# One transfer for the first load, and the last values ahead of the fold, in an adaLN decode block with cached attention

## The chip, the cores and the metric

The kernel runs on one core of a Trainium2 chip. The metric is the device time of one execution in microseconds (us), the median of several runs.

## The reference

Two decode tokens (B = 2, one position each) of width 512 go through an adaLN block: attention over a cache of 4096 keys with 32 heads of 128, then a dense layer with Mish, both behind a layer norm that is scaled and shifted by a condition `c`. Cut to what matters:

```python
mod = (silu(c) @ w_mod).reshape(2, 6, 1, 512)          # w_mod: 512 x 3072
sa, ca, ga, sb, cb, gb = (mod[:, i] for i in range(6))
h = layernorm(x) * (1 + ca) + sa
q = (h @ wq)                                            # wq: 512 x 4096, 32 heads of 128
scores = einsum("bhqd,bhkd->bhqk", q, k_cache) * 128 ** -0.5
o = einsum("bhqk,bhkd->bhqd", softmax(scores), v_cache) # caches: 2 x 32 x 4096 x 128
x = x + ga * (o @ wo)                                   # wo: 4096 x 512
h = layernorm(x) * (1 + cb) + sb
x = x + gb * (mish(h @ w1 + b1) @ w2)                   # w1: 512 x 1376, w2: 1376 x 512
```

Everything is float32. The caches alone are 268 MB; all that is read once is 297 MB.

## The kernel before

**The loads.** Nearly all input comes in 36 loads, which `stream` lays out ahead of time: each is one or more transfers into a "room", a tile of 128 partitions x 16384 floats (8 MB, 64 KB a partition). There are three rooms (`bufs=3`), so load n + 3 has to wait until a room has been read. Loads 1 to 31 are one transfer each, with rows of 64 KB: the keys of a head and, in what room is left, values and projection weights. Load 0 holds the weights of modulations 0 and 1, the first two query projections and the keys of head 0; it is two transfers with rows of 32 KB, weights first. Load 32 has values of head 28, the last `wo` pieces and modulation 2's weights; load 33 the values of heads 29 and 30; load 34 modulation 4's weights and the values of head 31 in three transfers; load 35 the weights of modulations 3 and 5, `w1` and `w2` in six transfers, cut so that the last `w2` chunks come in small pieces. All loads go through SyncE's queue (SP), in this order, issued by `load` (L140); `used` calls it when everything in an older room has been used.

**Three small transfers** go through ScalarE's queue at the start: `cq` (the condition, L162), `xq` (x, L162; eight rows of 512 B each) and `bias` (b1 in columns, L164; 128 rows of 48 B).

**The start.** On TensorE (PE), in program order: `cps` (c turned into columns, L237), the two sums of the first layer norm (L210, L218), `fps` (L269: the bias b1 put into PSUM, where the hidden layer is added at the very end), modulations 0 and 1 (L247), `hps` (L237), and the first two query projections (L294). The engine works strictly in that order.

**The middle.** For each of 32 heads VectorE (DVE) multiplies the keys by the query in place (`products`, L321) and sums over 128 (`sums`, L324), 64 keys a partition; PE and ScalarE (ACT) make the soft-max and PE multiplies by the values (`weighted_v`, L362), with four groups of 32 rows side by side. After four heads `value_sums`, `head_values` and `project_o` bring the result through `wo` into `att`.

**The tail.** Behind the last head: the values of heads 29 and 30, then `project_o` for all but head 31, a copy of `att` to SBUF (`att_sb`, L470), the first half of head 31's values, the fold (L474: four 32-row groups brought together into `xps`), modulation 4, kept by ACT through `keep`, the second half of the values, their way through `value_sums`, `head_values` and `head_out_q` (L401), which adds head 31 into `xps`. Then x is updated (L490, L493), the second layer norm follows (`centred`, `rstd`), modulation 3, `w1` (L514), Mish, modulation 5 and `w2` (`yps`, L554). `busy(n)` (L301) is n idle matmuls of 128 columns, which only keep PE going.

The order on each engine is the order of the program: there is no planner.

Of the kernel before, what the change touches and what calls it, by code (L numbers as in the profile page):

```python
# [9 lines left out]
AF = mybir.ActivationFunctionType  # L10
ALU = mybir.AluOpType
# [7 lines left out]
BIG = 8192  # L19
W = 2048  # L20
# [6 lines left out]
ROW = 2 * BIG  # L27


def stream():  # L30


    order, n_v = [], 0
    for h in range(1, HEADS):
        order.append(("k", h))
        if h % HC == HC - 1 and HC < h < HEADS - 1:
            c = (h + 1) // HC
            order.append([("wq", c), ("wo", c - 2)])
        if h not in AHEAD:
            order += [("v", n_v, 0), ("v", n_v, 1)]  # L40
            n_v += 1
    order = [x if isinstance(x, list) else [x] for x in order]

    def size(x):
        return sum(SIZES[key[0]] for key in x)

    loads = [[([("m01", 0), ("wq", 0), ("wq", 1)], (4 * W,)), ([("k", 0)], (BIG,))]]
    for _ in range(1, HEADS):
        row = []
        while size(row) < ROW:  # L50
            room = ROW - size(row)
            row += order.pop(next(i for i, x in enumerate(order) if size(x) <= room))
        loads.append([(row, (ROW,))])
    last = [("v", h, i) for h in range(HEADS - 4, HEADS) for i in range(2)]
    assert order == [[key] for key in last[:2]], order
    loads += [
        [(last[:2] + [("wo", 6), ("wo", 7), ("m2", 0)], (BIG + 3 * W,))],
        [(last[2:4], (BIG,)), (last[4:6], (BIG,))],
        [([("m4", 0)] + last[6:], (W + HALF, W, W))],
        [  # L60
            ([("m3", 0), ("w1", 0)], (W + 2 * sum(WIDTHS), 2 * sum(WIDTHS))),
            ([("m5", 0), ("w2", 0)], (W + 5 * 512, 4 * 512, 512, 512)),
        ],
    ]
    return loads
# [3 lines left out]
def kernel(  # L69
# [15 lines left out]
    nc = tc.nc  # L85
# [7 lines left out]
    H = HEADS  # L93
# [12 lines left out]
    def small_ps(name):  # L106
        return psum.tile([P, 512], F32, tag="sm", name=name, bufs=2)

    def wide_ps(name):
        return psum.tile([P, 512], F32, tag="mm", name=name, bufs=2)  # L110
# [19 lines left out]
    w_t = {}  # L130
# [14 lines left out]
    def used(*keys):  # L145

        nonlocal loaded
        done.update(keys)
        while loaded < len(loads) and (
            loaded < 3 or all(key in done for keys, _ in loads[loaded - 3] for key in keys)  # L150
        ):
            load(loaded)
            loaded += 1
# [6 lines left out]
    for t, src in ((cq, head[0]), (xq, head[1])):  # L160
        nc.gpsimd.memset(t, 0.0)
        nc.scalar.dma_start(out=t[::TB, :], in_=src)  # L162
    bias = const.tile([P, NCH + 1], F32, name="bias")
# [7 lines left out]
        out=fold, in_=ident.rearrange("p (g r) -> p r g", g=G), axis=AX.X, op=ALU.add  # L171
# [3 lines left out]
        out=mean_w, in0=fold[:, None, :].to_broadcast([P, G, R]), scalar1=1.0 / D, scalar2=None, op0=ALU.mult  # L175
# [4 lines left out]
        out=half, in_=ident.rearrange("p (b r) -> p r b", b=B), axis=AX.X, op=ALU.add  # L180
# [19 lines left out]
    def centred(src, name, first_sum=None, between=None):  # L200

        rs = const.tile([P, 8], F32, name=f"rs_{name}")
        xc = work.tile([P, P], F32, tag="xc", name=f"xc_{name}", bufs=1)
        sq = work.tile([P, P], F32, tag="sq", name=f"sq_{name}", bufs=1)
        if first_sum is None:
            nc.vector.tensor_reduce(out=rs[:, 0:1], in_=src, axis=AX.X, op=ALU.add)
        else:
            first_sum(rs[:, 0:1])
        mps = small_ps(f"mean_{name}")
        nc.tensor.matmul(mps[:, 0:1], lhsT=mean_w, rhs=rs[:, 0:1], start=True, stop=True)  # L210
        nc.vector.tensor_scalar(out=xc, in0=src, scalar1=mps[:, 0:1], scalar2=None, op0=ALU.subtract)
        nc.vector.scalar_tensor_tensor(
            sq, xc, 1.0, xc, op0=ALU.mult, op1=ALU.mult, accum_out=rs[:, 1:2]
        )
        if between is not None:
            between()
        vps = small_ps(f"var_{name}")
        nc.tensor.matmul(vps[:, 0:1], lhsT=mean_w, rhs=rs[:, 1:2], start=True, stop=True)  # L218
        return xc, vps[:, 0:1], rs
# [20 lines left out]
    def modulation(name, n, t, ps=None, ks=range(G)):  # L240


        if ps is None:
            ps = wide_ps(f"modps{name}")[:, : n * P].rearrange("p (m n) -> p m n", m=n)
        for k in ks:
            for g in range(G):
                nc.tensor.matmul(  # L247
                    ps[R * g : R * (g + 1)],
                    lhsT=ct[:, k, :],
                    rhs=t[:, k, :].rearrange("p (m n) -> p m n", m=n)[:, :, P * g : P * (g + 1)],  # L250
                    start=(k == 0),
                    stop=(k == G - 1),
                )
        return ps
# [9 lines left out]
    xc, var, rs = centred(xq, "a")  # L264
# [10 lines left out]
    mod = {}  # L275

    def keep(m, ps):
        mod[m] = const.tile([P, P], F32, name=f"mod{m}")
        nc.scalar.copy(mod[m], ps)
# [17 lines left out]
    def busy(n):  # L297

        for lo in range(0, n, 2):
            cols = P * min(2, n - lo)  # L300
            nc.tensor.matmul(ov[1][:, :cols], lhsT=ident, rhs=e_t[0].rearrange("p c m -> p (c m)")[:, :cols], start=True, stop=True)  # L301
# [56 lines left out]
    def weighted_v(h, part, bank, first=True, last=True):  # L358

        for c in range(NB // 2):  # L360
            g = c % G
            nc.tensor.matmul(  # L362
                ov[bank][R * g : R * (g + 1), :],
                lhsT=e_t[h % HC][:, NB // 2 * part + c, :],
                rhs=v_t[h, part][:, c, :],
                start=(first and part == 0 and c < G),
                stop=(last and part == 1 and c >= NB // 2 - G),
            )
        used(("v", h, part))

    def value_sums(bank, copies):

        o_t.clear()
        n = 4 // len(copies)
        for i, copy in enumerate(copies):
            o = work.tile([P, 4, DH], F32, tag="o", name=f"o{bank}")[:, :n]
            copy(o.rearrange("p m d -> p (m d)"), ov[bank][:, n * DH * i : n * DH * (i + 1)])  # L377
            for m in range(n):
                o_t[n * i + m] = o[:, m, :]

    def head_values(n, i0=0, i1=HC):
        x = slice(B * i0, B * i1)
        tps = small_ps(f"otp{n}_{i0}")
        for m in range(4):
            nc.tensor.matmul(  # L385
                tps[:, x], lhsT=o_t[m], rhs=pick_t[n][:, m, x], start=(m == 0), stop=(m == 3),
            )
        nc.scalar.copy(ot_t[n % 2][:, i0:i1, ::TB], tps[:, x].rearrange("p (i b) -> p i b", b=B))
# [9 lines left out]
    def head_out_q(h):  # L398

        for g in range(G):  # L400
            nc.tensor.matmul(  # L401
                xps[R * g : R * (g + 1), :P],
                lhsT=ot_t[h // HC % 2][:, h % HC, :],
                rhs=wo_t[h // HC][:, h % HC, P * g : P * (g + 1)],
                start=False, stop=(h == H - 1), skip_group_check=True,
            )
# [51 lines left out]
    N = H // HC - 1  # L458
# [10 lines left out]
    att_sb = work.tile([P, 512], F32, tag="o", name="att_sb")  # L469
    nc.scalar.copy(att_sb, att)  # L470
    xps = psum.tile([P, 512], F32, tag="att", name="xps", bufs=1)
    weighted_v(H - 1, 0, 1 - N % 2)
    for g in range(G):
        nc.tensor.matmul(  # L474
            xps[R * g : R * (g + 1), :P], lhsT=fold, rhs=att_sb[:, P * g : P * (g + 1)],
            start=True, stop=False, skip_group_check=True,
        )
    keep(4, modulation("4", 1, w_t["m4"])[:, 0, :])
    weighted_v(H - 1, 1, 1 - N % 2)
    value_sums(1 - N % 2, (nc.scalar.copy, nc.vector.tensor_copy))  # L480
    busy(2)
    head_values(N, HC - 1, HC)
    busy(1)
    head_out_q(H - 1)
    wm3, wm5 = w_t["m3"], w_t["m5"]
    w1_t, w2_t = w_t["w1"], w_t["w2"]

    xg = work.tile([P, P], F32, tag="sq", name="xg", bufs=1)
    x2 = const.tile([P, P], F32, name="x2")
# [3 lines left out]
        nc.vector.scalar_tensor_tensor(x2, xg, 1.0, xq, op0=ALU.mult, op1=ALU.add, accum_out=total)  # L493

    m4 = work.tile([P, P], F32, tag="xn", name="m4", bufs=1)
    busy(2)
    xc, var, rs = centred(x2, "b", add_x, lambda: busy(4))
    mps3 = modulation("3", 1, wm3)
    busy(1)
    nc.vector.scalar_tensor_tensor(m4, mod[4], 1.0, xc, op0=ALU.add, op1=ALU.mult)  # L500
    y0, y1 = rstd(var, rs)
    nc.scalar.activation(xc, m4, AF.Copy, scale=y0)
    nc.vector.scalar_tensor_tensor(hq, xc, y1, mps3[:, 0, :], op0=ALU.mult, op1=ALU.add)
# [63 lines left out]
def _lay_out(np, a):  # L567
# [39 lines left out]
    for n, parts in enumerate(stream()):  # L607
        for i, (keys, widths) in enumerate(parts):
            row = np.concatenate([piece(*key) for key in keys], axis=1)
            cuts = np.split(row, np.cumsum(widths)[:-1], axis=1)  # L610
            for j, t in enumerate(cuts):
                arrays[f"load{n}_{i}_{j}"] = np.ascontiguousarray(t)
# [25 lines left out]
```

## Time and profile before

| what | value |
|---|---|
| time, median of 3 runs | 698.67 us (698.63 to 698.77) |
| the profiled execution's own time | 698.77 us |
| its span | 696.9 us |
| busy: PE / DVE / ACT / POOL | 41% / 84% / 6% / 1% |
| DMA | 297.48 MB in 6690 packets, mean 427 GB/s |
| mean granted clock of PE | 0.677 |

The profile is of one execution; its span runs from the first instruction to the last, and the execution's own time is 1.9 us longer. Times in the lines are microseconds from the span's start, unless marked as nanoseconds. In a timeline a line has the start, the duration, the engine, the line of the kernel, the operation, the tile written and the tiles read, the count, and in brackets the idle time before it with what ended it; PEld is the weight load of PE, and SPq and ACTq are the queues of DMA issues. "DMA to landing" is the time from a transfer's issue to its last completion. In a line of a window (`A:B`) stand its length, the busy time of PE, PEld, DVE, ACT and POOL with counts, then the granted clock of PE, the DMA share and GB/s.

### The profile page before, as it was taken

To read this page: it belongs to the slowest core of one execution; us is meant where nothing else is said; L and a number is where in the kernel's file an instruction comes from. 1 tells how busy PE (TensorE), PEld (TensorE's weight loads), DVE (VectorE), ACT (ScalarE), POOL (GpSimd) and SP (SyncE) were. 2 spreads that over 40 slices of the span, in tenths; PEclk is the share of its full clock that TensorE was granted. 3 is DMA by queue.
4 is the path that set the end of the run, shared out by engine and by line. 5 is a ranking of instruction groups with operands and counts; after the bars stand their busy time and mean duration, and the time that the engine had idled before them with its cause. 6 is when DMAs were issued, how large, how long until landed. Compare 5 with 4: busy or idle time off the path is not lost.

```text
span 696.9 us, 3922 instructions
## 1 busy us (share of the span) xinstructions
PE 284.6 (41%) x1640; PEld 103.9 (15%) x1640; DVE 587.1 (84%) x219; ACT 44.3 (6%) x169; POOL 4.2 (1%) x20
## 2 busy tenths in 40 slices
PE   0603334335145615234342806234333425224697
PEld 0200011001011201101110301011101111001245
DVE  3399999999999999999999999999999999899002
ACT  1000000000000000000000000000000000000011
POOL 2000000000000000000000000000000000000000
PEclk9966656768565567656575656656575658556889
DMA  9999999999999999999999999999999999999996
GB/s 388 455 421 421 425 467 429 418 430 425 463 422 421 437 421 456 429 421 441 421 451 429 418 444 425 448 426 421 441 429 445 429 421 441 429 434 422 425 419 266
DMA packets 6690, 297.48 MB, mean 427 GB/s; under 512 B 888, under 2 KB 912, under 8 KB 1168
## 3 DMA queue, kind: packets, MB, share of 16 engines
q1 hardware_dynamic: 6496, 297.21, 98.9%
q8 instruction: 13, 0.21, 0.1%
q10 hardware_dynamic: 176, 0.01, 0.0%
q14 instruction: 5, 0.04, 0.0%
HBM read 297.22 MB, written 0.00 MB: 426 GB/s over the span
## 4 chain that ended last, share of the span: by engine, by line
DMA 63%; DVE 33%; PE 2%; issue 0%; SPq 0%; POOL 0%; ACT 0%; ACTq 0%; DVEq 0%; POOLq 0%
DMA room<-in_load 61%; DVE room L321 16%; DVE s L324 16%; DMA bias<-in_b1c 3%; PE ov L362 1%; PE qps L294 1%; PE modps L247 1%; PE yps L554 0%; SPq L140 0%; DVE m L337 0%; DVE hcw L283 0%; DVE m L329 0%; PE fps L269 0%; ACT q L295 0%; ACTq L162 0%
## 5 line engine op out<-in xcount | busy, mean ns | idle before, releaser
L321 DVE TENSOR_TENSOR room<-room,q 128x8192 f32<-128x8192 f32 x32 | 278.1, 8691 | 40.0 <-DMA room<-in_load 35.5
L324 DVE TENSOR_REDUCE s<-room 128x64 f32<-128x8192 f32 x32 | 277.9, 8683 | 0.0
L362 PE MATMUL ov<-room,e 128*32 128x512 f32 x1024 | 177.0, 841 | 73.5 <-ACT e L340 31.2
L333 PE MATMUL mt<-d,same 128*128 128x64 f32 x64 | 18.7, 388 | 194.0 <-DVE d L331 194.0
L362 PEld LDWEIGHTS ov<-room,e 128*32 128x32 f32 x1024 | 39.8, 146 | 180.8 <-issue 128.3
L340 ACT ACTIVATE e<-s,m 64x64 f32<-64x64 f32 x64 | 22.1, 345 | 547.9 <-DVE m L337 547.1
L333 PEld LDWEIGHTS mt<-d,same 128*128 128x128 f32 x64 | 13.5, 263 | 224.6 <-DVE d L331 177.6
L294 PE MATMUL qps<-room,hcw 128*128 128x512 f32 x64 | 40.7, 797 | 4.6 <-DMA room<-in_load 3.8
L348 PE MATMUL l<-l,ones 128*128 128x8 f32 x16 | 4.6, 359 | 73.7 <-ACT e L340 73.7
L385 PE MATMUL otp<-pick,o 128*128 128x8 f32 (+2 forms) x72 | 14.4, 328 | 37.3 <-ACT o L377 35.4
L377 DVE COPY o<-ov 128x256 f32<-128x256 f32 x1 | 0.4, 423 | 25.1 <-ACT o L377 25.1
L385 PEld LDWEIGHTS otp<-pick,o 128*128 128x128 f32 x72 | 13.6, 282 | 46.6 <-ACT o L377 43.7
L294 PEld LDWEIGHTS qps<-room,hcw 128*128 128x128 f32 x64 | 15.9, 261 | 24.4 <-issue 18.6
L348 PEld LDWEIGHTS l<-l,ones 128*128 128x128 f32 x16 | 3.8, 296 | 75.1 <-ACT e L340 75.1
L393 PE MATMUL att<-room,ot 128*32 128x512 f32 x62 | 10.9, 756 | 5.2 <-DMA room<-in_load 4.7
L337 DVE TENSOR_REDUCE m<-mt 128x1 f32<-128x64 f32 x32 | 6.9, 217 | 6.3 <-PE mt L333 6.3
L340 ACT ACTIVATION_READ_ACCUMULATOR e<-s,m 64x1 f32 x64 | 11.8, 185 | 0.0
L331 DVE TENSOR_SCALAR d<-half,m 128x64 f32<-128x64 f32 x32 | 8.1, 254 | 1.1
L273 DVE SCALAR_TENSOR_TENSOR hq<-modps,xn 128x128 f32<-128x128 f32 x1 | 0.3, 291 | 10.4 <-PE modps L247 10.4
L247 PE MATMUL modps<-room,ct 128*32 128x128 f32 (+1 forms) x160 | 8.1, 346 | 0.0
L329 DVE TENSOR_REDUCE m<-s 128x1 f32<-128x64 f32 x32 | 6.9, 217 | 0.9
L377 ACT COPY o<-ov 128x512 f32<-128x512 f32 (+1 forms) x9 | 5.1, 562 | 24.2 <-PE ov L362 24.1
(100 smaller groups left out, 68.5 us busy)
## 6 DMA issues: line engine op xcount, KB each, us to landing
room<-in_load SPq DMA_DIRECT2D x4, 4096.0 KB, 28.5
room<-in_load SPq DMA_DIRECT2D x1, 7168.0 KB, 39.1
room<-in_load SPq DMA_DIRECT2D x1, 3072.0 KB, 26.1
room<-in_load SPq DMA_DIRECT2D x3, 1024.0 KB, 22.3
room<-in_load SPq DMA_DIRECT2D x1, 2400.0 KB
room<-in_load SPq DMA_DIRECT2D x1, 2304.0 KB, 20.3
room<-in_load SPq DMA_DIRECT2D x1, 1376.0 KB, 15.2
room<-in_load SPq DMA_DIRECT2D x2, 256.0 KB, 22.6
```

The costliest lines, as they stand in the source:

```text
L247: nc.tensor.matmul(ps[R * g : R * (g + 1)], lhsT=ct[:, k, :], rhs=t[:, k, :].rearrange("p (m n) -> p m n", m=n)[:, :, P * g : P * (g + 1)] ...
L294: nc.tensor.matmul(ps, lhsT=hcw[:, k, :], rhs=wq_t[ch][:, k, :], start=(k == 0), stop=(k == G - 1))
L321: nc.vector.tensor_tensor(out=k_t[h], in0=k_t[h], in1=qv, op=ALU.mult)
L324: nc.vector.tensor_reduce(out=s_t[h], in_=k_t[h], axis=AX.X, op=ALU.add)
L329: nc.vector.tensor_reduce(out=m_t[h][:, 0:1], in_=s_t[h], axis=AX.X, op=ALU.max)
L331: nc.vector.tensor_scalar(out=d, in0=half, scalar1=m_t[h][:, 0:1], scalar2=None, op0=ALU.mult)
L333: nc.tensor.matmul(mps[h], lhsT=same, rhs=d, start=True, stop=True)
L340: nc.scalar.activation(e_t[i][own_b, :, M * i + 4 * b : M * i + 4 * b + 4], s_t[h][own_b].rearrange("p (c m) -> p c m", m=4), AF.Exp, bias ...
L348: nc.tensor.matmul(lps[n], lhsT=ones, rhs=sum_t[n % 2], start=True, stop=True)
L362: nc.tensor.matmul(ov[bank][R * g : R * (g + 1), :], lhsT=e_t[h % HC][:, NB // 2 * part + c, :], rhs=v_t[h, part][:, c, :], start=(first a ...
L385: nc.tensor.matmul(tps[:, x], lhsT=o_t[m], rhs=pick_t[n][:, m, x], start=(m == 0), stop=(m == 3),)
L393: nc.tensor.matmul(att[R * i : R * (i + 1), :], lhsT=ot_t[n % 2][:, i, :], rhs=wo_t[n][:, i, :], start=(n == 0), stop=(n == H // HC - (2 i ...
```

## The change

Two things are changed. Load 0 becomes a single transfer with rows of 64 KB, in the same order of content. In the tail both halves of head 31's values are multiplied one after the other, and `value_sums` follows at once; the fold comes behind them. Modulation 4 moves behind that and is cut in two: k = 0 and 1 ahead of `head_out_q`, k = 2 and 3 behind it, where idle matmuls stood. It is no longer kept in SBUF as such: ACT writes 1 + modulation straight into `m4`, and DVE multiplies that by the centred x. Of the idle matmuls of 128 columns in the part shown here, 5 remain (1 + 3 + 1) of 10 (2 + 1 + 2 + 4 + 1).

```diff
-    loads = [[([("m01", 0), ("wq", 0), ("wq", 1)], (4 * W,)), ([("k", 0)], (BIG,))]]
+    loads = [[([("m01", 0), ("wq", 0), ("wq", 1), ("k", 0)], (ROW,))]]
...
-    weighted_v(H - 1, 0, 1 - N % 2)
+    for part in range(2):
+        weighted_v(H - 1, part, 1 - N % 2)
+    value_sums(1 - N % 2, (nc.scalar.copy, nc.vector.tensor_copy))
     for g in range(G):
         nc.tensor.matmul(
             xps[R * g : R * (g + 1), :P], lhsT=fold, rhs=att_sb[:, P * g : P * (g + 1)],
             start=True, stop=False, skip_group_check=True,
         )
-    keep(4, modulation("4", 1, w_t["m4"])[:, 0, :])
-    weighted_v(H - 1, 1, 1 - N % 2)
-    value_sums(1 - N % 2, (nc.scalar.copy, nc.vector.tensor_copy))
-    busy(2)
+    busy(1)
     head_values(N, HC - 1, HC)
-    busy(1)
+    mps4 = modulation("4", 1, w_t["m4"], ks=(0, 1))
     head_out_q(H - 1)
+    modulation("4", 1, w_t["m4"], mps4, (2, 3))
...
     m4 = work.tile([P, P], F32, tag="xn", name="m4", bufs=1)
-    busy(2)
-    xc, var, rs = centred(x2, "b", add_x, lambda: busy(4))
+    nc.scalar.activation(m4, mps4[:, 0, :], AF.Copy, bias=1.0)
+    xc, var, rs = centred(x2, "b", add_x, lambda: busy(3))
     mps3 = modulation("3", 1, wm3)
     busy(1)
-    nc.vector.scalar_tensor_tensor(m4, mod[4], 1.0, xc, op0=ALU.add, op1=ALU.mult)
+    nc.vector.tensor_tensor(out=m4, in0=xc, in1=m4, op=ALU.mult)
     y0, y1 = rstd(var, rs)
```

## The prediction

> **What bounds the kernel now.** I read the page first, for the engines and the DMA by slices, then the chain that ended last, then the timeline of the first 50 us and of the last 35.
>
> ```profile
> DMA  9999999999999999999999999999999999999996
> GB/s 388 455 421 421 425 467 429 418 430 425 463 422 421 437 421 456 429 421 441 421 451 429 418 444 425 448 426 421 441 429 445 429 421 441 429 434 422 425 419 266
> q1 hardware_dynamic: 6496, 297.21, 98.9%
> DMA 63%; DVE 33%; PE 2%; issue 0%; SPq 0%; POOL 0%; ACT 0%; ACTq 0%; DVEq 0%; POOLq 0%
> ```
>
> The DMA engines are busy in every slice but the last, all 297 MB on SP's queue. The 33% of DVE in the chain misleads; a stretch of the chain in order of time (start, duration, what) shows why:
>
> ```profile
> 102.08 38.23 DMA room<-in_load
> 140.34 8.69 DVE room L321
> 149.13 8.70 DVE s L324
> 157.83 0.02 SPq L140
> 157.89 40.51 DMA room<-in_load
> 198.42 8.69 DVE room L321
> ```
>
> A load of 8 MB is issued when DVE has read a room (157.83) and lands two load times later (198.40), because another load is still ahead of it. Three loads land between 140.31 and 198.40, one every 19.36 us, while DVE needs 17.4 us and a little for a head. So the stream of loads is the bound, and a load's issue matters only if the queue ahead of it has run dry. That leaves two places to look at: whether the queue can run dry, and what follows the last landing.
>
> **Part 1, the first load as one transfer of 64 KB rows.** Its own bytes are the same. These rows show the start: SP's loads, the queues in the first 25 us, two windows (the last number is GB/s), and the timeline up to the first pass of DVE.
>
> ```profile
> L140 SPq DMA_DIRECT2D room<-in_load x4: 392/422/495, 0.7 to 2.1; - x4
> DMA to landing us min/median/max: 21.6/40.5/59.4
> ```
>
> ```profile
> DMA packets 496, 10.50 MB, mean 420 GB/s; under 512 B 192, under 2 KB 208, under 8 KB 208
> q10 hardware_dynamic: 176, 0.01, 0.5%
> ```
>
> ```profile
> 0.00:5.00 5.00, 0.00 (x0) 0.00 (x0) 3.14 (x8) 1.28 (x1) 3.83 (x19) 1.00 0.70 249
> 15.00:20.00 5.00, 0.00 (x0) 0.00 (x0) 0.00 (x0) 0.00 (x0) 0.00 (x0) 1.00 1.01 433
> ```
>
> ```profile
> 0.97 1.17 ACTq L162 DMA_DIRECT2D cq<-in_head  x1
> 2.17 0.58 ACTq L162 DMA_DIRECT2D xq<-in_head  x1
> 2.79 0.45 ACTq L164 DMA_DIRECT2D bias<-in_b1c  x1
> 8.23 0.56 PE L237 MATMUL cps<-ident,cq 128*128 128x8 f32 x2 [8.23 <-DMA cq<-in_head]
> 10.57 0.29 DVE L206 TENSOR_REDUCE rs_a<-xq 128x1 f32<-128x128 f32 x1 [0.81 <-DMA xq<-in_head]
> 20.40 0.62 PE L269 MATMUL fps<-bias,ident 128*128 128x24 f32 x2 [7.54 <-DMA bias<-in_b1c]
> 20.95 3.64 PE L247 MATMUL modps<-room,ct 128*32 128x256 f32 x32
> 30.87 8.69 DVE L321 TENSOR_TENSOR room<-room,q 128x8192 f32<-128x8192 f32 x1 [4.42 <-ACT q L295]
> 39.60 8.69 DVE L324 TENSOR_REDUCE s<-room 128x64 f32<-128x8192 f32 x1
> ```
>
> The row to see is L269. PE stands for 7.5 us before the bias matmul, and what it waits for is 6 KB that ACT issued at 2.79. That matmul stands ahead of modulation 0 on PE, and behind that come the first projections and DVE's first pass: all of it hangs on `bias`.
>
> Why do 6 KB take 17.6 us? 433 GB/s over 16 engines is 27.1 GB/s each, so a 32 KB row of the first load holds an engine for 1.21 us. `xq` (one row of 512 B on an engine, and a completion) lands 2.34 us after `cq`, which is 1.17 a packet; `bias` (128 rows, so eight on each engine, and a completion) lands 9.83 after `xq`, 1.09 a packet. The 176 packets of q10 fit this count: 128 rows of bias, 16 of `cq` and `xq`, 32 completions. So each small packet on ACT's queue waits for about one row of SP's queue; that the mean is under 1.21 fits one step of the eleven which fell beside the completion of the first half of load 0 and cost nothing.
>
> With 64 KB rows such a step is 2.42 us. From `cq` to `bias` there are eleven, ten of them paid (load 0's completion still falls among them): 24.2 us. For `cq` itself I have bounds only. Data starts at about 2.1 us (249 GB/s over 5 us is 2.9 us of work at 433), so `cq` landed five packet times after it. If all five double it lands at 14.3, if only its own row and its completion do, at 10.6. I take four, 8.2 + 4 x 1.21 = 13.0: ACT's issue ended at 2.14, when data had hardly begun, so nearly all of the five stood ahead of `cq`, but part of the first is start-up and not row. `bias` then lands at 13.0 + 24.2 = 37.2, against 20.4: **16.8 us later**. Ends: 14.4 (`cq` at 10.6) and 20.5 (`cq` at 14.3, no free step). As the least, with `cq` where it is now and ten steps of 2.42, it is 12.0.
>
> By the Trainium skill's page "DMA: Bandwidth & Descriptors", section "Queues, rings and completion order", an engine goes round its queues by packets, and a packet typically holds 9 to 17 descriptors. By that, the nine small ones of `bias` would go in one turn, which here would have been at about 12 us; the trace has 20.4, so the turn is one row here and the measurement decides.
>
> Load 0 itself lands at about 22.8 as now (min 21.6 from an issue near 1.2), well ahead of the new `bias`; before, its first half was there earlier, but PE did not use it before 20.95, so that loss costs nothing. The PE and DVE work from 20.40 to 30.87 is unchanged and moves whole.
>
> What is queued behind: DVE's first pass starts at 47.7 and its sums end at 48.3 + 16.8 = **65.1**, which is when SP can issue load 3 into room 0 (as at 157.83, the issue follows the sums at once). Load 2, issued at 2.1, lands 59.4 later: **61.5**. The cover was 13 us and is gone. An issue into an empty queue pays the start-up as well: load 0 was issued at 0.74 and landed at 22.8, 22.1 us, against 19.36 in the stream, so 2.7 us. The stream loses 65.1 + 2.7 - 61.5 = **6.3 us**. With the shift at 14.4, 20.5 and 12.0 it loses 3.9, 10.0 and 1.5.
>
> A second dry spot does not follow: load 3 lands at 65.1 + 22.1 = 87.2 and load 4 is issued one head after load 3, at 83. DVE then gains about 1.4 us a head on the stream, and nothing behind gives the 6.3 us back, since the stream bounds all the rest.
>
> Saved: one issue on SP (0.4 us, off the path) and one boundary between two transfers. The boundary has no price to be seen: inside the second half of load 0 the rate is 433 GB/s, which is 19.37 us for 8 MB, and whole loads, each with its boundary, take 19.36.
>
> **Part 2, the tail.** These rows are the end: PE from the last values on, SP's last issues, and what PE waits for at `yps`; then the load that the chain has there, and two lines of the DMA issues (KB each, us to landing).
>
> ```profile
> 667.68 2.97 SPq L140 DMA_DIRECT2D room<-in_load  x6
> 673.01 0.50 PE L474 MATMUL xps<-att_sb,fold 128*32 128x128 f32 x2
> 674.09 1.00 PE L247 MATMUL modps<-room,ct 128*32 128x128 f32 x28
> 675.03 1.89 PE L362 MATMUL ov<-room,e 128*32 128x512 f32 x15
> 678.40 0.47 PE L301 MATMUL ov<-e,ident 128*128 128x128 f32 x2
> 679.15 0.70 PE L301 MATMUL ov<-e,ident 128*128 128x256 f32 x2
> 681.45 1.08 PE L247 MATMUL modps<-room,ct 128*32 128x128 f32 x32
> 690.19 1.27 PE L554 MATMUL yps<-room,actt 128*32 128x128 f32 x40
> 691.65 1.74 PE L554 MATMUL yps<-room,actt 128*32 128x128 f32 x48 [0.18 <-DMA room<-in_load]
> ```
>
> ```profile
> 669.29 22.31 DMA room<-in_load
> ```
>
> ```profile
> room<-in_load SPq DMA_DIRECT2D x3, 1024.0 KB, 22.3
> room<-in_load SPq DMA_DIRECT2D x2, 256.0 KB, 22.6
> ```
>
> The fold (L474) and modulation 4 stand between the two halves of the last values from 673.01 to about 675.1. Put behind them, the values can start up to 2.0 us earlier (675.0 to 673.0), or not at all earlier if the last columns of `v` land only then: 0 to 2.0, and I take the middle, 1. Modulation 4 is 1.08 us by its twin at 681.45; cut in two it takes 0.54 where the idle matmul of 0.47 stood, beside ACT's copy, and 0.54 behind the last output where 0.70 of idle matmuls stood. On PE that is even. On DVE the product at L500 becomes a product of the same shape, on ACT one scaling takes the place of the copy: even.
>
> What that 1 us is worth is read at `yps`. Its first 40 matmuls end at 691.46, PE waits 0.18 for the transfer issued at 669.29 (691.60), and the last eight need one issued at about 670.25 that lands 22.6 later, 692.85, when PE has just done the 40 before. The six issues of load 35 stay where they are: they wait for the values of heads 29 and 30, done at 667.68, which the change doesn't touch. So the last landings are set by the stream, a tail that is earlier only waits longer, and the gain is **0**. Bounds: 0.2 us gained (all of that wait), and 1.8 lost if the wait for `v` comes to stand ahead of the fold with nothing to do (2.0 less the 0.2); I take 0, which the 0.18 is nearest to. If the stream were no longer last here, the whole 1 us would show.
>
> Sum: 6.3 + 0 = 6.3 us. The profiled execution took 698.77 (span 696.9 and 1.9 around it), so 705.1, and against the median of 698.67, **705.0 us**.
>
> **The rivals.** What can be told from no change here is about 0.2%, 1.4 us.
>
> *Colder PE besides.* The first projections now run at full clock after 4 us of warm modulation. PE's granted clock fell as soon as it idled (0.84 in the stretch below, with no PE work in it). If it is at half all through the moved stretch, the eight matmuls ahead of the first q (3.71 us in the chain, 26.50 to 30.22) take 3.7 more, all of it on load 3's issue: 705.0 + 3.7 = 708.7. Against it: modulation 0 was itself preceded by idle time, and the projections behind it ran warm. 0.09.
>
> ```profile
> 35.00:40.00 5.00, 0.00 (x0) 0.00 (x0) 4.97 (x2) 0.00 (x0) 0.00 (x0) 0.84 0.97 419
> 26.50 3.71 PE qps L294 x8
> ```
>
> *The queue does not run dry.* If the small packets don't wait for whole 64 KB rows (turns of a fixed size in bytes, or several small rows in a turn), `bias` moves little; below a shift of 61.5 - 2.7 - 48.3 = 10.5 us nothing is lost: 698.7, no change. The Trainium skill's rule above is of this kind. For it: no trace here shows a small queue beside 64 KB rows. Against it: 1.17 and 1.09 us a packet with 32 KB rows, close to a row and to nothing else. 0.12.
>
> *Faster: a transfer has a fixed cost.* One transfer fewer at the head of the stream shortens everything behind it, if the second one began only when the first was complete. The price is at most the start-up worked out above, 2.7 us less the 0 of a queued boundary: 696.0; it decides only if `bias` moves by less than 10.5 us. Against it stand 433 GB/s inside a transfer and the same across boundaries. 0.04. [...]
>
> **How the numbers follow.** The main case has 0.75. Slower: 0.75 + 0.09 = 0.84; same 0.12; faster 0.04. The range runs from 701.0, between the least shift (700.2) and the one at 14.4 (702.6), to 708.7, where the high end of the shift (10.0) and the cold PE both come out. It leaves out the two rivals that are not slower, 0.16, and little of the main case.
>
> **What would show it.** Right: `bias` releases L269 near 37, DVE's first pass starts near 47.7, SP issues load 3 near 65 with load 2 landed at 61.5; the slice from 52 to 70 us falls from 421 to about 270 GB/s; later loads still come every 19.36 us; at the end PE waits longer than 0.18 at `yps`. Wrong: `bias` still near 20 (then 698.7), or near 37 with no dip in GB/s; or a tail in which `yps` no longer waits for the load.

## The result and the profile after

The changed kernel takes **704.27 us** (median of 6 runs, 702.15 to 705.63) against 698.72 (6 runs, 698.63 to 699.05): ratio 1.0074, 95% interval 1.0063 to 1.0085, slower. The profiled execution is one of the shorter ones, 702.49 us with a span of 700.7. Forecast were 705.0 and a range of 701.0 to 708.7.

The page of the changed kernel, the DMA by slices and the chain:

```profile
DMA  9998999999999999999999999999999999999996
GB/s 420 419 419 359 419 419 454 441 417 426 449 435 419 431 441 435 426 430 427 453 423 430 427 453 423 423 439 445 426 419 435 453 426 420 434 442 414 424 421 264
q1 hardware_dynamic: 6352, 297.21, 98.4%
DVE 48%; DMA 48%; PE 2%; issue 0%; SPq 0%; POOL 0%; ACT 0%; ACTq 0%; DVEq 0%; POOLq 0%
```

The fourth slice (52.5 to 70 us) is the one that changed: 359 GB/s where 421 stood. Behind it the stream is as fast as before. DVE's share of the chain has grown from 33% to 48%, and it stands at the front: DVE does not wait for a load from its first pass until it has caught up with the stream, at 279.8 us where it was 121.0; from there on a head takes 19.4 us in both kernels.

The timeline of the start, from the small loads to the sums of head 0:

```profile
10.44 0.57 PE L237 MATMUL cps<-ident,cq 128*128 128x8 f32 x2 [10.44 <-DMA cq<-in_head]
15.18 0.29 DVE L206 TENSOR_REDUCE rs_a<-xq 128x1 f32<-128x128 f32 x1 [3.21 <-DMA xq<-in_head]
34.62 0.62 PE L269 MATMUL fps<-bias,ident 128*128 128x24 f32 x2 [17.15 <-DMA bias<-in_b1c]
35.17 3.64 PE L247 MATMUL modps<-room,ct 128*32 128x256 f32 x32
45.10 8.69 DVE L321 TENSOR_TENSOR room<-room,q 128x8192 f32<-128x8192 f32 x1 [4.42 <-ACT q L295]
53.83 8.69 DVE L324 TENSOR_REDUCE s<-room 128x64 f32<-128x8192 f32 x1
```

L269 waits 17.15 us for the bias in place of 7.54, and all behind it has moved by 14.2 us. The next rows are SP's issue of loads 3 and 4, the landing time of load 3 (the one line for the window from 50 to 84 us) and of the first three loads (window from 0 to 50), and the traffic in steps of 6 us:

```profile
62.59 18.18 SPq L140 DMA_DIRECT2D room<-in_load  x2
```

```profile
DMA to landing us min/median/max: 21.7/21.7/21.7
DMA to landing us min/median/max: 21.8/40.7/59.6
```

```profile
54.00:60.00 6.00, 0.00 (x0) 0.00 (x0) 6.00 (x1) 0.00 (x0) 0.00 (x0) 0.50 0.81 350
60.00:66.00 6.00, 0.69 (x2) 0.50 (x2) 5.93 (x4) 0.00 (x0) 0.00 (x0) 0.50 0.50 175
66.00:72.00 6.00, 0.00 (x0) 0.00 (x0) 6.00 (x3) 0.11 (x1) 0.00 (x0) 0.50 1.21 524
```

Load 3 is issued at 62.59, 1.3 us after load 2 has landed (the last of three issues between 0.74 and 2.1, so near 1.7, and 59.6 later: 61.3), and lands 21.7 later, at 84.3. In a full stream it would have landed at 61.3 + 19.36 = 80.7. The stream has lost **3.6 us** in this execution, and its time is 3.7 above the profiled one of before. The bytes of a row seem to be counted where it starts: the first sixteen rows of 64 KB stand in the record by 2.4 us, though their load was issued at 0.74 and a row takes 2.42. So windows of 6 us swing even in a full stream. The kernel before has 350 and 524 in the same two windows, and 175 is below both:

```profile
54.00:60.00 6.00, 1.34 (x8) 0.45 (x12) 6.00 (x3) 0.88 (x4) 0.00 (x0) 0.50 0.81 350
60.00:66.00 6.00, 4.05 (x28) 0.94 (x20) 6.00 (x1) 0.00 (x0) 0.00 (x0) 0.81 1.21 524
```

The tail of the changed kernel, modulation 5 and `w2`:

```profile
693.38 1.08 PE L247 MATMUL modps<-room,ct 128*32 128x128 f32 x32 [0.63 <-DMA room<-in_load]
695.60 1.03 PEld L554 LDWEIGHTS yps<-room,actt 128*32 128x32 f32 x40 [0.32 <-DMA room<-in_load]
696.94 0.16 PEld L554 LDWEIGHTS yps<-room,actt 128*32 128x32 f32 x8 [0.30 <-DMA room<-in_load]
```

PE still waits for load 35, now at modulation 5 too.

Two things were open. Which half of the change costs what; and why the six times lie 3.5 us apart where the kernel before has 0.4.

### The profile page after: what moved, and what is told of

Same layout as the page of the kernel before. It is cut to its first block, busy times and chain, and to the rows that moved or that the text cites. A ratio compares the mean times of both kernels' runs of the same rounds, so it can differ in the third digit from the quotient of the medians.

```text
span 700.7 us, 3914 instructions
## 1 busy us (share of the span) xinstructions
PE 281.0 (40%) x1636; PEld 102.6 (15%) x1636; DVE 586.5 (84%) x219; ACT 44.3 (6%) x169; POOL 4.3 (1%) x20
## 4 chain that ended last, share of the span: by engine, by line
DVE 48%; DMA 48%; PE 2%; issue 0%; SPq 0%; POOL 0%; ACT 0%; ACTq 0%; DVEq 0%; POOLq 0%
DMA room<-in_load 43%; DVE s L324 24%; DVE room L321 23%; DMA bias<-in_b1c 5%; PE ov L362 1%; PE qps L294 1%; PE modps L247 1%; DVE d L331 0%; DVE m L329 0%; PE yps L554 0%; SPq L140 0%; DVE m L337 0%; DVE hcw L283 0%; PE fps L269 0%; ACT q L295 0%
## 5 line engine op out<-in xcount | busy, mean ns | idle before, releaser
L362 PE MATMUL ov<-room,e 128*32 128x512 f32 x1024 | 175.0, 834 | 67.9 <-ACT e L340 28.4
L385 PE MATMUL otp<-pick,o 128*128 128x8 f32 (+2 forms) x72 | 14.2, 325 | 37.1 <-ACT o L377 35.3
L340 ACT ACTIVATION_READ_ACCUMULATOR e<-s,m 64x1 f32 x64 | 11.8, 185 | 0.0
L269 PE MATMUL fps<-bias,ident 128*128 128x24 f32 x2 | 0.6, 397 | 17.1 <-DMA bias<-in_b1c 17.1
## 6 DMA issues: line engine op xcount, KB each, us to landing
room<-in_load SPq DMA_DIRECT2D x1, 2304.0 KB, 20.4
```

Of the source, the lines that this page charges most:

```text
L340: nc.scalar.activation(e_t[i][own_b, :, M * i + 4 * b : M * i + 4 * b + 4], s_t[h][own_b].rearrange("p (c m) -> p c m", m=4), AF.Exp, bias ...
L362: nc.tensor.matmul(ov[bank][R * g : R * (g + 1), :], lhsT=e_t[h % HC][:, NB // 2 * part + c, :], rhs=v_t[h, part][:, c, :], start=(first a ...
L385: nc.tensor.matmul(tps[:, x], lhsT=o_t[m], rhs=pick_t[n][:, m, x], start=(m == 0), stop=(m == 3),)
```

## The experiments

**Load 0 alone.** The kernel before with only the first line of the change.

```diff
-    loads = [[([("m01", 0), ("wq", 0), ("wq", 1)], (4 * W,)), ([("k", 0)], (BIG,))]]
+    loads = [[([("m01", 0), ("wq", 0), ("wq", 1), ("k", 0)], (ROW,))]]
```

> Only load 0 as one transfer; the tail as before. Theory (small packets wait for 64 KB rows, bias comes late, the stream runs dry): all of the 5.6 us is here, about 704.3, L269 released at 34.6 or one turn of 2.4 us later, DVE's first pass from about 45 on. Rival (the tail's new order costs some of it): clearly under 704, near 699 if all.

Measured: 703.6 us (4 runs, 702.48 to 706.12), ratio 1.0069 (1.0051 to 1.0087). L269 started at 34.78, DVE's first pass at 45.26. Within the scatter of the runs all of the loss is here.

**The tail alone.** The changed kernel with the old line for load 0.

```diff
-    loads = [[([("m01", 0), ("wq", 0), ("wq", 1), ("k", 0)], (ROW,))]]
+    loads = [[([("m01", 0), ("wq", 0), ("wq", 1)], (4 * W,)), ([("k", 0)], (BIG,))]]
```

> Only the tail changed; load 0 as two transfers of 32 KB rows. Theory (the stream sets the end, an earlier tail only waits): 698.7, within 0.3 us, with the last w2 transfers landing when they do before. Rival (the tail's order matters by itself): 697.6 if the 1 us taken for the earlier values shows, or about 700.5 if the wait for v now stands bare.

Measured: 698.86 us (11 runs) against 698.97 (21 runs), ratio 0.9998 (0.9989 to 1.0007). Its timeline shows where the gain stays:

```profile
682.61 2.77 PE L514 MATMUL w1ps<-room,h2t 128*32 128x384 f32 x32
689.10 1.08 PE L247 MATMUL modps<-room,ct 128*32 128x128 f32 x32 [0.93 <-DMA room<-in_load]
691.50 1.74 PE L554 MATMUL yps<-room,actt 128*32 128x128 f32 x48 [0.23 <-DMA room<-in_load]
```

The kernel before has:

```profile
683.80 2.77 PE L514 MATMUL w1ps<-room,h2t 128*32 128x384 f32 x32
```

So `w1` begins 1.2 us earlier. SP's last issues are 0.26 earlier in this execution (667.42, before 667.68), which leaves about 0.9 for the tail itself; which of its edits gives that was not told apart. PE then waits 0.93 at modulation 5 for weights that land at 689.1, and again at `yps`, which begins its last 48 matmuls at 691.50 in place of 691.65.

The start of this kernel is that of the kernel before, and yet two of its lines differ:

```profile
26.09 8.83 PE L294 MATMUL qps<-room,hcw 128*128 128x512 f32 x16 [0.78 <-DVE hcw L283]
32.16 8.69 DVE L321 TENSOR_TENSOR room<-room,q 128x8192 f32<-128x8192 f32 x1 [6.12 <-ACT q L295]
```

The first projections took 8.83 us where the kernel before has 7.13, and DVE's first pass came 11.8 us behind the start of L269 (20.36) in place of 10.5. This execution took 698.66 us, so the delay cost nothing here.

**The bias matmul behind the projections.** The changed kernel, where PE reaches the matmul that waits for `bias` only when the first queries are on their way.

```diff
-    nc.tensor.matmul(fps, lhsT=ident, rhs=bias[:, :, None].to_broadcast([P, NJ * G, B]), start=True, ...)
...
     project_q(0)
     project_q(1)
+    nc.tensor.matmul(fps, lhsT=ident, rhs=bias[:, :, None].to_broadcast([P, NJ * G, B]), start=True, ...)
```

> The changed kernel, single transfer and all, but the bias matmul (L269 before) moved behind the first two query projections on PE, so that nothing early waits for bias. Theory: bias still lands near 34 to 37, but modulation 0 starts when load 0 lands, near 22.8, DVE's first pass at about 33, the stream stays full: 698.7. Rival (the single transfer itself is the cost, by slower rows or a later landing): stays near 704.

Measured: 698.55 us (11 runs, 698.41 to 698.95), ratio 0.9993 (0.9985 to 1.0002) to the kernel before. Modulation 0 now waits for load 0 and for nothing else:

```profile
22.95 3.51 PE L247 MATMUL modps<-room,ct 128*32 128x256 f32 x32 [5.45 <-DMA room<-in_load]
28.36 8.83 PE L293 MATMUL qps<-room,hcw 128*128 128x512 f32 x16 [0.78 <-DVE hcw L282]
34.42 8.69 DVE L320 TENSOR_TENSOR room<-room,q 128x8192 f32<-128x8192 f32 x1 [6.12 <-ACT q L294]
```

The single transfer by itself costs nothing. What costs is what waited behind it on the other queue, and PE's order that made all else wait for that. The second line shows the long projections once more: 8.83 us here and 7.13 in the changed kernel.

**The changed kernel once more**, for a second look at the start.

> The changed kernel once more, for a second profile of the start; its six times lay at 702.2 to 705.6. Theory A of that spread (the first small packet gets in one 64 KB row earlier or later): cq, xq and bias all 2.4 us later or not, times 702.3 or 704.7. Theory B (the first projections run on a PE whose clock has or hasn't risen yet): bias at 34.6 in all, the time from L269 to DVE's first pass 10.5 us or up to 3.7 more.

Measured: 702.35 us, L269 at 34.77, DVE's first pass at 45.24. It was one of the short executions, so it does not tell the two theories apart.

**Idle matmuls ahead of the bias**, first 21 of them, then 33, to have PE's clock up when the bias lands.

```diff
+    for _ in range(33):      # 21 in the first of the two
+        nc.tensor.matmul(ov[1][:, : 2 * P].rearrange("p (a b) -> p a b", a=2), lhsT=ident, rhs=ident[:, None, :].to_broadcast([P, 2, P]), start=True, stop=True)
     nc.tensor.matmul(fps, lhsT=ident, rhs=bias[:, :, None].to_broadcast([P, NJ * G, B]), start=True, ...)
```

> The changed kernel with 21 idle matmuls of 256 columns put on PE between the first layer norm and the bias matmul, so that PE is running, and its clock up, when bias lands; they write nothing that is used. Theory B of the spread (202.2 to 206.1 above 500 us over the changed kernel and the one with load 0 alone: projections sometimes on a half clock): modulation 0 takes 1.8 us in place of 3.64, DVE's first pass starts near 43.3, the stream loses 1.9 us, median 700.7 and all times within about 0.7 us. Theory A (the small packets get in a row earlier or later): the median falls by the 1.8 us too, but the spread stays 2.4 us or more.

Measured: 703.26 us (6 runs, 702.12 to 705.44), ratio 1.0064 (1.0052 to 1.0076), which did not settle it:

```profile
17.33 11.78 PE L270 MATMUL ov<-ident 128*128 128x256 f32 x42
34.62 0.62 PE L271 MATMUL fps<-bias,ident 128*128 128x24 f32 x2 [5.51 <-DMA bias<-in_b1c]
35.17 3.64 PE L247 MATMUL modps<-room,ct 128*32 128x256 f32 x32
```

The idle work ended 5.5 us early and modulation 0 took the same 3.64 us as without it. The granted clock stood at 0.50 over 34 to 38 us here. The changed kernel's row for that stretch, the first of these two, says 1.00, with the same 3.64 us for the same matmuls:

```profile
34.00:38.00 4.00, 3.38 (x30) 1.88 (x34) 0.00 (x0) 0.00 (x0) 0.00 (x0) 1.00 1.10 475
38.00:42.00 4.00, 2.48 (x13) 0.98 (x6) 1.28 (x3) 0.00 (x0) 0.00 (x0) 1.00 1.21 524
```

So the granted clock can't be read from such rows this early in the changed kernel, and the time of the matmuls decides. The longer one:

> As the kernel with 21 idle matmuls, which ended at 29.1 with 5.5 us of idle time before the bias matmul, so that the clock had fallen again: now 33 of them, which at 0.43 us until the clock is up and 0.217 a matmul behind that end near 34.5. Theory B of the spread (projections on half the clock in some executions): modulation 0 takes 1.8 us in place of 3.64, DVE's first pass starts near 43.3, median about 700.6, all times within about 0.7 us. Theory A (small packets get in a 64 KB row earlier or later): median 1.8 us lower too, and a spread of 2.4 us or more as now.

Measured: **700.89 us** (6 runs, 700.56 to 701.91), ratio 1.0029 (1.0018 to 1.0041).

```profile
17.63 16.69 PE L270 MATMUL ov<-ident 128*128 128x256 f32 x66
34.92 0.40 PE L271 MATMUL fps<-bias,ident 128*128 128x24 f32 x2 [0.60 <-DMA bias<-in_b1c]
35.25 1.93 PE L247 MATMUL modps<-room,ct 128*32 128x256 f32 x32
39.09 7.13 PE L296 MATMUL qps<-room,hcw 128*128 128x512 f32 x16 [0.78 <-DVE hcw L285]
43.46 8.69 DVE L323 TENSOR_TENSOR room<-room,q 128x8192 f32<-128x8192 f32 x1 [4.42 <-ACT q L297]
```

`bias` lands when it did, the median falls by 3.4 us, more than the 1.7 that modulation 0 gives, and the spread falls from 3.5 us to 1.35. The small packets were not moved, so theory A would have left the spread: about 2 us of it go when PE is kept running. Nor does any profile show theory A: in all eight with load 0 in 64 KB rows `cq` is read at 10.4 to 10.7 us. That the spread is not under 0.7 stays unexplained.

**Bias as 12 rows.** The changed kernel with the same 6 KB in another shape. A turn, here and below, is the wait of one small packet for one row of the bulk load.

```diff
-    bias = const.tile([P, NCH + 1], F32, name="bias")
+    bias = const.tile([NCH + 1, P], F32, name="bias")
...
-    nc.tensor.matmul(fps, lhsT=ident, rhs=bias[:, :, None].to_broadcast([P, NJ * G, B]), start=True, ...)
+    nc.tensor.matmul(fps, lhsT=bias, rhs=ident[: NJ * G, : NJ * G, None].to_broadcast([NJ * G, NJ * G, B]), start=True, ...)
```

> The changed kernel with b1 loaded as 12 rows of 512 B (a row on each of 12 engines) where it was 128 rows of 48 B, and turned into columns by the same matmul with the operands exchanged. Theory (each small packet waits for one 64 KB row): two turns behind xq in place of nine, so bias lands near 15.2 + 4.8 = 20, ahead of load 0; DVE's first pass at about 33, no dry stretch, 698.6. Rival (bias is late because 6 KB on a second queue is starved beside 64 KB rows, whatever its rows): L269 stays near 34.7 and the time near 703.5.

Measured: 698.75 us (11 runs), ratio 0.9997 (0.9989 to 1.0006).

```profile
20.12 0.61 PE L269 MATMUL fps<-ident,bias 12*128 12x24 f32 x2 [2.60 <-DMA bias<-in_b1c]
22.80 3.64 PE L247 MATMUL modps<-room,ct 128*32 128x256 f32 x32 [2.06 <-DMA room<-in_load]
```

The same bytes beside the same 64 KB rows land at 20.1, where the count of turns put them: four behind `cq` (10.50), 2.41 us each. All four lie ahead of load 0's landing and all are paid, which fits a free step that comes only with such a landing. It is the number of rows, not the bytes and not the queue.

**Load 0 with rows of 16 KB**, in four transfers.

```diff
-    loads = [[([("m01", 0), ("wq", 0), ("wq", 1), ("k", 0)], (ROW,))]]
+    loads = [[([("m01", 0), ("wq", 0), ("wq", 1), ("k", 0)], (ROW // 4,) * 4)]]
```

> The changed kernel with load 0 as four transfers with rows of 16 KB. Theory (a turn is one row of SP's queue): the step halves once more to 0.6 us, xq lands about 1.2 us after cq and bias 5 to 5.5 after xq, near 13; DVE's first pass then waits for the first loads alone, about 25 to 31; time 698.7, as before. Rival (a turn is a fixed number of bytes or microseconds that 32 KB happens to fill): bias again near 20.

Measured: 699.37 us (10 runs) against 698.93, ratio 1.0006 (0.9997 to 1.0015), no difference that this can tell.

```profile
13.47 0.62 PE L269 MATMUL fps<-bias,ident 128*128 128x24 f32 x2 [2.41 <-DMA bias<-in_b1c]
62.10 8.69 DVE L321 TENSOR_TENSOR room<-room,q 128x8192 f32<-128x8192 f32 x1 [0.61 <-DMA room<-in_load]
```

`bias` near 13, as the turns say: 13.5, 20.4 and 34.6 us with rows of 16, 32 and 64 KB. DVE begins 5 us earlier than in the kernel before, and by its third head it waits for the stream: an earlier start is worth nothing here.

**More turns.** The changed kernel with a further small transfer ahead of `bias`.

```diff
+    spare = const.tile([P // 2, NCH + 1], F32, name="spare")
+    nc.scalar.dma_start(out=spare, in_=b1c[: P // 2])
     nc.scalar.dma_start(out=bias, in_=b1c)
```

> The changed kernel with one more small transfer on ACT's queue ahead of bias: 64 rows of 48 B, four on each engine and a completion, read by nobody. Theory (each packet waits for one 64 KB row, and the stream is dry from load 2's landing to load 3's issue): bias 5 x 2.42 = 12.1 us later, L269 at 46.7, and all of it on the time: 702.4 to 706 becomes 714.5 to 718. Rival (the stream has other slack): less than 12 us more.

Measured: **714.24 us** (4 runs, 712.37 to 714.96), ratio 1.0215 (1.0199 to 1.0231), 10.0 above the changed kernel's median. Timeline, then the first q in the chain, the granted clock by windows (the third number from the end), and the dry stretch:

```profile
44.44 0.62 PE L271 MATMUL fps<-bias,ident 128*128 128x24 f32 x2 [26.87 <-DMA bias<-in_b1c]
56.45 8.69 DVE L323 TENSOR_TENSOR room<-room,q 128x8192 f32<-128x8192 f32 x1 [6.12 <-ACT q L297]
```

```profile
50.39 5.41 PE qps L296 x8
```

```profile
46.00:50.00 4.00, 2.86 (x30) 1.14 (x22) 0.94 (x3) 0.00 (x0) 0.00 (x0) 1.00 1.17 508
50.00:54.00 4.00, 3.61 (x6) 1.66 (x7) 0.34 (x1) 0.00 (x0) 0.00 (x0) 0.70 1.21 524
54.00:58.00 4.00, 4.00 (x9) 1.68 (x9) 1.55 (x1) 0.60 (x1) 0.00 (x0) 0.88 0.64 279
```

```profile
60.00:66.00 6.00, 0.00 (x0) 0.00 (x0) 5.97 (x2) 0.00 (x0) 0.00 (x0) 0.65 0.00 0
66.00:72.00 6.00, 0.00 (x0) 0.00 (x0) 6.00 (x1) 0.00 (x0) 0.00 (x0) 0.50 0.00 0
```

3 KB that nobody reads cost 10 us. L269 is 9.8 later than in the changed kernel's profile, not 12.1: four steps of 2.42 are 9.7. The fifth would be one that fell beside load 1's completion, as one of the eleven falls beside load 0's; I had not allowed for that in the count, and no view here shows the single step. The profiled execution took 713.54, 11.05 above the changed kernel's; DVE's first pass is 11.35 later, of which 1.7 is the first q (5.41 against 3.71) on a clock that had fallen. So the landing of `bias` goes into the time about one to one, and here the fallen clock is seen in the same trace as its cost.

## Why the prediction was right

**The chain of causes** came out as it was put: PE held by `bias`, `bias` by the rows of the other queue, DVE by PE, load 3 by DVE, and the stream dry between load 2's landing and load 3's first bytes. Two experiments take away one link each and get all of the loss back: the matmul moved (698.55) and the rows of `bias` fewer (698.75). A third adds turns and nearly triples the loss (714.24).

**The step** of 2.42 us and the count of ten paid ones were right: from `cq` to `bias`, by the matmuls that wait for them (10.44 and 34.62), are 24.2 us, forecast 24.2. The Trainium skill's page "DMA: Bandwidth & Descriptors", section "Queues, rings and completion order", has an engine change queues at packets of typically 9 to 17 descriptors; with 16, 32 and 64 KB rows here a turn was one row each time, and the runs decide.

**The term that was mis-sized is `cq`.** I took 13.0, four steps behind its place of before; it landed at 10.44, at the low end of 10.6. The argument that nearly all five packet times stood ahead of it as rows was wrong: with rows of 16, 32 and 64 KB `cq` is read at 7.34, 8.23 and 10.44 us, so about two rows' time grows with the rows and some 6 us do not; what those are made of no run shows. So the shift was 14.2 and not 16.8, and with 14.2 the prediction's own sum gives 48.3 + 14.2 + 2.7 - 61.5 = 3.7 us; the profiled execution has 3.7. The start-up of an empty queue, put at 2.7, measured 21.7 - 19.36 = 2.3. The slice fell to 359 GB/s, not 270, since the dry stretch was that much shorter.

**The median is nevertheless close to 705.0**, and that is luck in part: two errors stand against each other. The sum is 2.6 us too high for the short execution that was profiled, and it left out what makes other executions longer. What I had as a rival with 0.09, the colder PE, is, as far as the runs tell, no rival but a part of some executions. The changed kernel's times go from 702.2 to 705.6; with PE kept running they are 700.6 to 701.9. That the same start can have short and long projections is seen in the kernel before (7.13) and in the run with the tail alone (8.83), and the last experiment shows such a delay in its time (the first q at 5.41 in place of 3.71). All profiles of the changed kernel itself and of the one with load 0 alone are of short executions with short projections, so in the long ones it was not seen: it is shown by taking it away, not by a trace of it. No profile has more than 1.7 us of delay from it, less than the spread of 3.5, so the rest of the spread stays open.

The rival's price and its reading of the clock were off too. It put 3.7 us on the first q, where 1.7 is the most seen, and it said that the clock falls as soon as PE idles: in the kernel before PE's last matmul ends at 33.6 us, and the granted clock stays at 1.00 up to 38 and is 0.59 over 38 to 40. Nor was modulation 0 warm: it took 3.64 us, and 1.93 behind the long run of idle matmuls.

The Trainium skill's page "TensorE: Matmul & The Clock Gate", section "Part 1: The HAM clock gate", says that the clock rises after some 3.4 us of sustained work in a window that runs free of the kernel's start, so that the number of cold matmuls differs from run to run. That fits: the two shares of 0.70 and 0.88 in the last experiment make 2.4 and 1.0 us at half clock, 3.4 together; that the window runs free no trace here shows. The page puts the ramp under 1% of a span, and the whole spread, 3.5 of 704 us, is within that, though here it is more than half of the loss. With the start of the kernel before, the same delay costs nothing (698.66 in the run with the tail alone), since the stream has 13 us to spare there.

**The tail at 0** was right: 0.9998, with about 0.9 us won at `w1` (I took 1) and given back at modulation 5 and `yps`. **The rival "the queue does not run dry"** fell with the step of 2.42, and **the fixed cost of a transfer** with the single transfer at 698.55 when nothing waits for `bias`: 2.7 us less would have been 696.0.

No version beats the kernel before beyond its interval: the matmul moved (0.9985 to 1.0002) and the 12 rows (0.9989 to 1.0006) both come back to the stream's own length.

## What to carry to other kernels

Beside this stream a small transfer paid about one bulk row for each of its own rows on an engine. Where the same shows, count (rows / 16, rounded up, + 1) x the time of a bulk row, less a step where a bulk load completes meanwhile, and give small tensors few long rows. Look in the program order for what waits behind such a landing, and put a matmul that is needed only at the end behind the work that feeds the pipeline. In a kernel bound by its loads as this one is, a late start costs nothing until the queue runs dry, and from there on it costs about one to one; find that point before pricing anything else.

## What the runs showed of the hardware

Rows of 16, 32 and 64 KB on one queue put the same 6 KB on another queue at 13.5, 20.4 and 34.6 us. PE's clock fell without a long pause too: after a stretch with 2.86 us of work in 4 it was taken down in the next (granted 0.70 over 50 to 54 us). The amount of work alone does not decide it: the changed kernel had 2.48 us of work over 38 to 42 us, and its projections behind that took the short 7.13. A pause of 5.5 us undid 11.8 us of idle matmuls. An issue into an empty queue landed 2.3 us later than one into a full stream would have taken.
